# A top-k attention kernel whose fold takes one operand of its maximum from PSUM, with the second heads' keys stored tail first

## The chip, the cores and the metric

The kernel runs on one core of one Trainium2 chip. The metric is the device time of one execution in microseconds. Before the change the median of three runs is 1749.21 us (1747.92 to 1749.37). The engines are called as the profile calls them: PE (TensorE, matmuls; PEld is its weight load), DVE (VectorE), ACT (ScalarE), POOL (GpSimd) and SP (the queue that issues the transfers).

## The reference

Eight batches of eight heads, 576 positions, head size 64, fp32. The first block is attention that keeps the 32 largest scores of each row; the second is a mixer over positions of rank 32, and an MLP of width 2048 over channels.

```
scores = scale * q @ k.T
kth    = np.partition(scores, -32, axis=-1)[..., -32:-31]
scores = np.where(scores >= kth, scores, -1e9)
attn   = softmax(scores)                     # sum + 1e-9 below
x      = (attn @ v), heads side by side      # (8, 576, 512)
u      = x + (x.T @ U @ V).T
out    = u + relu(u @ w_ch1) @ w_ch2
```

## The kernel before, in words

**Pairs and chunks.** Two heads make a pair: 32 pairs `g`, four of each batch. A pair's 576 query rows are cut into five chunks `t`: four of 128 rows, in which both heads' scores lie side by side (2 x 576 columns), and a tail, in which the 64 last rows of one head stand above those of the other (576 columns). That gives 160 steps `n`. The positions of a head are kept as 512 (`MAIN`) and 64 (`TAIL`); `HALF` is 288.

**Loads.** `load(g)` fetches q, k and v on SP. From the sixth pair on (`blocked(g)`, `g > 4`) q and k are laid down in blocks of 32 so that one DVE transpose of 32 x 32 blocks, L290, makes `qkT` (heads on the two halves of the partitions, positions along the columns). Earlier pairs are turned by PE.

**Scores.** `scores(g, t)` multiplies by halves of 288 keys. A chunk of 128 rows uses two PSUM tiles `sc` of two banks each (L335, four matmuls): the first holds keys 0 to 287 of both heads, the second 288 to 575. Three ACT copies (L346, L347, L348) move them to `Ssb`, since head one's 64 last keys are put ahead of its first 512: head nought lies at columns 0 to 575, head one's tail at 576 to 639, its rest behind it. A tail chunk takes one tile, four matmuls of 64 rows (L323) and one copy (L330). `ps_s` has two such tiles in all, so a chunk's scores wait until the readers of the chunk before have let go of the tiles.

**The fold.** From the fifth pair on `fold` and `split` (both through `pair`) cut the search in two: POOL adds the two halves of each head's row as 32-bit words (L370), DVE takes their maximum (L372, `upper`), POOL subtracts that from the sum (L373), which leaves the minimum (`lower`). `front` then searches both: the 16 largest of `lower` join `upper` (L412 to L416), and `upper`, 304 wide, gives the 32 largest by MAX8 and MATCH_REPLACE8 (L426, L438, L443).

**After the search.** ACT makes `gap` (L468), POOL subtracts it (L471) so that what is under the threshold falls away, ACT takes the exponential and its sum (L377). For PV the probabilities have to be turned: in the first chunks by PE (`turns`, L526, L531), later by DVE in blocks (L498) and a way through DRAM, `away`, back as `PT` (L504, L508); `values` multiplies (L560, L564, L550). `mixed` applies the rank-32 mixer (L596, L608, L610), and `mlp` the two MLP products (L633, L652).

**What sets the order.** The program is written out by hand for all engines, and each engine runs its list in order. The MLP of one batch is a list of fillers: `fill()` puts a measured share of its matmuls between the attention's steps of the next batches. In a step `n` the scores and the POOL addition of `n + 1` come first, DVE's maximum for `n + 1` (`split`) after two rounds of the search for `n`, then the blocks of `n - 1`; PE's products with V follow in the step after. The weights arrive as 64-bit words and are joined meanwhile, by ACT (L174 to L178), DVE (L186) and POOL (L187, L189), up to about 310 us.

Of the kernel before, what the change touches and what calls it, by code (L numbers as in the profile page):

```python
# [12 lines left out]
ALU = mybir.AluOpType  # L13
# [13 lines left out]
def kernel(  # L27
# [28 lines left out]
    nc = tc.nc  # L56
    B, H, S, D = q.shape
# [5 lines left out]
    NT, TAIL = 4, 64  # L63
    MAIN = NT * P
    HALF = S // 2
# [10 lines left out]
    BLK = 32  # L76
# [49 lines left out]
    def rows(t):  # L126
        return P if t < NT else TAIL

    def cols(t):
        return slice(t * P, t * P + rows(t))  # L130
# [4 lines left out]
    def half(h):  # L135
        return slice(h * D, (h + 1) * D)
# [77 lines left out]
    raws, parts, passes = [], [], []  # L214
# [17 lines left out]


    raw, qkTs, S2s, uTs, XTs, dens = {}, {}, {}, {}, {}, {}
    probs, PTs, folds = {}, {}, {}

    def load(g):
        b, h0 = g // NPAIR, 2 * (g % NPAIR)
        ld = loads.tile([P, 2 * S], F32, tag="ld", name="ld")
        if blocked(g):  # L240
            for i, src in enumerate((q, k)):
                for a in range(4):
                    ds = src[b, h0 + a // 2, :, a % 2 * BLK : (a % 2 + 1) * BLK]
                    to = ld[a * BLK : (a + 1) * BLK, i * S : (i + 1) * S]
                    nc.sync.dma_start(
                        to[:, 0:MAIN].rearrange("i (t m d) -> i t m d", t=NT, d=BLK),
                        ds[0:MAIN].rearrange("(m i t) d -> i t m d", i=BLK, t=NT),
                    )
                    nc.sync.dma_start(
                        to[:, MAIN:S].rearrange("i (m d) -> i m d", d=BLK),  # L250
                        ds[MAIN:S].rearrange("(m i) d -> i m d", i=BLK),
                    )
            raw[g] = ld
        else:
            tiles = []
            ends = ld[:, 2 * MAIN : 2 * S].rearrange("p (h d) -> p h d", h=2)
            for j, src in enumerate((q, k)):
                t = ld[:, j * MAIN : (j + 1) * MAIN].rearrange("p (t h d) -> p t h d", t=NT, h=2)
                for i in range(2):
                    queue = nc.scalar if g == 0 and i else nc.sync  # L260
                    queue.dma_start(
                        t[:, :, i, :],
                        src[b, h0 + i, 0:MAIN, :].rearrange("(p t) d -> p t d", t=NT),
                    )
                tiles.append(t)
            for i, src in enumerate((q, k)):
                nc.sync.dma_start(
                    ends[half(i)], src[b, h0 : h0 + 2, MAIN:S, :].rearrange("h p d -> p h d")
                )
            raw[g] = tiles, ends  # L270
        va, vd, vt = (a[g % NV] for a in (vas, vds, vts))
        for i in range(2):
            nc.sync.dma_start(
                va[:, i], v[b, h0 + i, 0:MAIN, :].rearrange("(p t) d -> p t d", t=NT)
            )
            nc.sync.dma_start(vd[half(i), half(i)], v[b, h0 + i, MAIN:S, :])
        nc.sync.dma_start(vt[TAIL:P], v[b, h0 : h0 + 2, MAIN:S, :].rearrange("h p d -> p h d"))

    def blocked(g):

        return g > NPAIR
# [26 lines left out]
    def scores(g, t):  # L310

        qkT = qkTs[g]
        S2 = attn.tile([P, 2 * (S + TAIL)], F32, tag="Ssb", name="Ssb", bufs=4)
        n = 2 if t < NT else 1
        probs[g, t] = S2
        S2s[g, t] = S2[:, 0 : n * S].rearrange("p (c n) -> p c n", c=n)
        if t == NT:
            sc = ps_s.tile([P, 2, 512], F32, tag="sc", name="sc")  # L320
            for i in range(2):
                for h in range(2):
                    nc.tensor.matmul(  # L323
                        sc[half(h), i, 0:HALF],
                        lhsT=qkT[half(h), 0, cols(t)],
                        rhs=qkT[half(h), 1, i * HALF : (i + 1) * HALF],
                        start=True,
                        stop=True,
                    )
            nc.scalar.copy(S2[:, 0:S].rearrange("p (i n) -> p i n", i=2), sc[:, :, 0:HALF])  # L330
            return
        scs = [ps_s.tile([P, 2, 512], F32, tag="sc", name="sc") for _ in range(2)]
        for i, sc in enumerate(scs):
            for h in range(2):
                nc.tensor.matmul(  # L335
                    sc[:, h, 0:HALF],
                    lhsT=qkT[half(h), 0, cols(t)],
                    rhs=qkT[half(h), 1, i * HALF : (i + 1) * HALF],
                    start=True,
                    stop=True,  # L340
                )

        main = S2.rearrange("p (h n) -> p h n", h=2)
        last = S2[:, MAIN : MAIN + 2 * TAIL].rearrange("p (h n) -> p h n", h=2)
        copy = nc.vector.tensor_copy if g + t == 0 else nc.scalar.copy
        copy(main[:, :, 0:HALF], scs[0][:, :, 0:HALF])  # L346
        nc.scalar.copy(main[:, :, HALF:MAIN], scs[1][:, :, 0 : MAIN - HALF])  # L347
        nc.scalar.copy(last, scs[1][:, :, MAIN - HALF : HALF])  # L348

    def fold(g, t):  # L350

        if NPAIR <= g < NP:
            upper = attn.tile([P, 2, HALF + TOPK // 2], F32, tag="upper", name="upper")
            lower = attn.tile([P, 2, HALF], F32, tag="lower", name="lower", bufs=1)
            folds[g, t] = upper, lower
            pair(g, t, 0)

    def split(g, t):

        if (g, t) in folds:  # L360
            pair(g, t, 1)

    def pair(g, t, stage):
        S2 = S2s[g, t]
        n = S2.shape[1]
        upper, lower = folds[g, t]
        top, bottom = upper[:, 0:n, 0:HALF], lower[:, 0:n].bitcast(U32)
        a, b = S2[:, :, 0:HALF], S2[:, :, HALF:S]
        if stage == 0:
            nc.gpsimd.tensor_tensor(bottom, a.bitcast(U32), b.bitcast(U32), ALU.add)  # L370
        else:
            nc.vector.tensor_tensor(top, a, b, ALU.max)  # L372
            nc.gpsimd.tensor_tensor(bottom, bottom, top.bitcast(U32), ALU.subtract)  # L373

    def weigh(chunk, E, nmax, total=None):
# [349 lines left out]
    def fill(k=1):  # L725
# [3 lines left out]
        for _ in range(k):  # L729
# [5 lines left out]
            while due > 0:  # L735
# [6 lines left out]
                else:  # L742
                    due -= done

    load(0)
    next_params(1)
    t = 0
    for _ in prep(0):
        pass
    scores(0, 0)  # L750
    turning = ready = iter(())
    fronts = {}
    for n in range(STEPS + 2):
        g, t = divmod(n, CH)
        if n < STEPS:
            if t == 0 and g + 1 < NP:
                load(g + 1)
            if t == 1 and g + 1 < NP:
                ready = prep(g + 1)
            fronts[n] = front(g, t)  # L760
            next(fronts[n])
        here, last = fronts.get(n, iter(())), fronts.pop(n - 1, iter(()))
        if n >= ALONE - 1 and n <= ALONE:

            if n < ALONE:
                next(last)
                values(*divmod(n - 3, CH))
                list(turning)
                next(here)
                next(last)  # L770
                scores(*divmod(n + 1, CH))
                fold(*divmod(n + 1, CH))
                values(*divmod(n - 2, CH))
            list(turns(*divmod(n - 1, CH)))
            values(*divmod(n - 1, CH))
            if n < ALONE:
# [7 lines left out]
                continue  # L784
            fill()
            scores(*divmod(n + 1, CH))
            fold(*divmod(n + 1, CH))
            next(here)
# [111 lines left out]
```

## Time and profile before

| | us |
|---|---|
| median of three runs | 1749.21 |
| profiled execution | 1745.95 |
| its span, first to last instruction | 1744.1 |
| PE busy | 1638.1 |
| DVE busy | 1515.5 |
| ACT busy | 1030.4 |
| POOL busy | 973.2 |

The span lies 1.85 us below the profiled execution's own time. The first 200 us are attention alone (the first batch), the last 140 the MLP of the last batch alone; between them all engines work on both. In the views below a group's line gives the engine, the operation, what it writes and reads, how often, its busy time and the mean of one in ns, and behind the second bar the engine's idle time ahead of it with what ended it. A line in order of time gives start and duration in us; the bracket at its end is the idle time before it and who ended it. A busy PE is not PE at its peak, because the ends of matmuls are modelled.

### The profile page before, as it was taken

The numbers are of one execution on the slowest core, as the hardware profiler recorded it, in microseconds if no ns is written. First come the engines' busy times: TensorE is split into PE (matmuls) and PEld (weight loads), VectorE is DVE, ScalarE is ACT, GpSimd is POOL, SyncE is SP. The second block draws the span as 40 slices with busy tenths as digits, with TensorE's granted clock in tenths as the row PEclk, the third lists the DMA queues.
The fourth block names the chain that finished last, engine by engine and source line by source line (L and its number), as shares of the span: only waits on it lengthen the run. The fifth ranks groups of instructions, "written<-read, shape, count | busy, mean of one in ns | idle before, by whom it ended". The sixth has DMA issues, their size and how long they took to land.

```text
span 1744.1 us, 29711 instructions
## 1 busy us (share of the span) xinstructions
PE 1638.1 (94%) x9435; PEld 1202.4 (69%) x9435; DVE 1515.5 (87%) x4358; ACT 1030.4 (59%) x2690; POOL 973.2 (56%) x759
## 2 busy tenths in 40 slices
PE   4576789999999999999999999999999999999999
PEld 2444556677667776678767776678767776678677
DVE  7999889899999999999999999999999999993000
ACT  4888787665656666565656656565656666563100
POOL 4778787656555555656555555656555555652000
PEclk7678899999999999999999999999999999999999
DMA  3332222344444443444444444444444444422010
GB/s 89 89 93 82 71 72 60 70 111 112 112 109 122 107 117 101 116 107 112 109 111 120 103 113 106 116 113 112 109 112 123 105 111 105 121 85 82 3 16 13
DMA packets 275837, 167.36 MB, mean 96 GB/s; under 512 B 173920, under 2 KB 260192, under 8 KB 275680
## 3 DMA queue, kind: packets, MB, share of 16 engines
q1 hardware_dynamic: 274624, 165.20, 36.4%
q8 instruction: 74, 1.21, 0.3%
q14 instruction: 83, 0.68, 0.1%
q10 hardware_dynamic: 1056, 0.26, 0.1%
HBM read 101.42 MB, written 63.96 MB: 95 GB/s over the span
## 4 chain that ended last, share of the span: by engine, by line
PE 73%; DVE 16%; ACT 3%; DMA 3%; POOL 3%; issue 2%; SPq 1%; POOLq 0%; DVEq 0%; ACTq 0%
PE mm L652 26%; PE mm L633 23%; PE sc L335 6%; PE O L564 6%; DVE m L443 5%; DVE hT L438 3%; DVE upper L438 2%; DMA PT<-away 2%; PE sc L323 2%; DVE first L426 2%; PE O L550 2%; PE up L608 1%; PE tp L531 1%; PE O L560 1%; PE tp L526 1%
## 5 line engine op out<-in xcount | busy, mean ns | idle before, releaser
L652 PE MATMUL mm<-hT,w 128*128 128x256 f32 (+1 forms) x2048 | 544.6, 410 | 0.7 <-ACT hT L645 0.7
L633 PE MATMUL mm<-uT,w 128*128 128x256 f32 (+1 forms) x2048 | 540.2, 411 | 0.0
L471 POOL TENSOR_TENSOR Ssb<-Ssb,E 128x576 f32<-128x576 f32 x271 | 379.4, 1418 | 270.5 <-ACT E L468 269.9
L633 PEld LDWEIGHTS mm<-uT,w 128*128 128x128 f32 x2048 | 376.1, 192 | 100.0 <-issue 13.3
L652 PEld LDWEIGHTS mm<-hT,w 128*128 128x128 f32 x2048 | 373.6, 192 | 95.2 <-issue 11.7
L443 DVE MAX8 m<-upper 128x8 f32<-128x304 f32 x756 | 323.9, 466 | 2.9
L373 POOL TENSOR_TENSOR lower<-lower,upper 128x576 uint32<-128x576 uint32 (+1 forms) x140 | 180.5, 1289 | 137.2 <-DVE upper L372 130.5
L377 ACT ACTIVATE Ssb<-Ssb,nmax 128x576 f32<-128x576 f32 x286 | 222.6, 783 | 17.2 <-POOL Ssb L448 9.2
L370 POOL TENSOR_TENSOR lower<-Ssb 128x576 uint32<-128x576 uint32 (+1 forms) x140 | 194.8, 1392 | 59.3 <-DVE first L426 18.3
L438 DVE MATCH_REPLACE8 upper<-m,upper 128x304 f32<-128x304 f32 x504 | 227.6, 459 | 0.0
L645 ACT ACTIVATE hT<-mm 128x320 f32<-128x320 f32 (+1 forms) x256 | 105.8, 413 | 201.1 <-PE mm L633 198.7
L468 ACT ACTIVATE E<-Ssb,least 128x576 f32<-128x576 f32 x271 | 197.9, 769 | 5.2
L335 PE MATMUL sc<-qkT 64*128 64x288 f32 x1024 | 167.7, 448 | 9.3 <-ACT Ssb L346 8.5
L564 PE MATMUL O<-PT,va 128*64 128x128 f32 x2048 | 144.4, 285 | 9.8 <-DMA PT<-away 9.5
L498 DVE STREAM_TRANSPOSE y<-Ssb 128x512 f32<-128x512 f32 x208 | 138.5, 694 | 8.2 <-ACT Ssb L377 7.4
L335 PEld LDWEIGHTS sc<-qkT 64*128 64x128 f32 x1024 | 91.9, 194 | 71.3 <-issue 27.8
L412 DVE MAX8 upper<-lower 128x8 f32<-128x288 f32 x252 | 103.0, 445 | 41.0 <-POOL lower L373 41.0
L372 DVE TENSOR_TENSOR upper<-Ssb 128x576 f32<-128x576 f32 (+1 forms) x140 | 123.7, 884 | 11.6 <-ACT Ssb L348 11.0
L564 PEld LDWEIGHTS O<-PT,va 128*64 128x64 f32 x2048 | 113.0, 140 | 27.0 <-DMA PT<-away 12.2
L665 DVE TENSOR_TENSOR oT<-uT,mm 128x320 f32<-128x320 f32 (+1 forms) x8 | 3.6, 455 | 140.8 <-PE mm L652 140.8
L346 ACT COPY Ssb<-sc 128x576 f32<-128x576 f32 x127 | 80.6, 635 | 71.4 <-PE sc L335 69.9
L573 ACT COPY XT<-O 128x128 f32<-128x128 f32 x128 | 34.2, 267 | 143.1 <-PE O L564 143.1
(95 smaller groups left out, 2233.8 us busy)
## 6 DMA issues: line engine op xcount, KB each, us to landing
away<-y SPq DMA_DIRECT2D x416, 128.0 KB, 2.4
PT<-away SPq DMA_DIRECT2D x104, 512.0 KB, 3.3
raw<-in_moe_w_ch_dram SPq DMA_DIRECT2D x32, 512.0 KB, 3.8
va<-in_v_dram SPq DMA_DIRECT2D x64, 128.0 KB, 2.2
out_dram<-ob SPq DMA_DIRECT2D x57, 128.0 KB, 2.0
ld<-in_q_dram SPq DMA_DIRECT2D x108, 64.0 KB, 2.6
ld<-in_k_dram SPq DMA_DIRECT2D x108, 64.0 KB, 2.3
ld<-in_q_dram SPq DMA_DIRECT2D x108, 8.0 KB, 2.2
```

What stands on the lines that cost most here:

```text
L335: nc.tensor.matmul(sc[:, h, 0:HALF], lhsT=qkT[half(h), 0, cols(t)], rhs=qkT[half(h), 1, i * HALF : (i + 1) * HALF], start=True, stop=True,)
L370: nc.gpsimd.tensor_tensor(bottom, a.bitcast(U32), b.bitcast(U32), ALU.add)
L373: nc.gpsimd.tensor_tensor(bottom, bottom, top.bitcast(U32), ALU.subtract)
L377: nc.scalar.activation(E, chunk, AF.Exp, bias=nmax, scale=SCALE, accum_out=total)
L438: nc.vector.match_replace(nxt, ms[c], curs[c], NEG)
L443: nc.vector.max(ms[c], curs[c])
L468: nc.scalar.activation(gap, chunks[c], AF.Relu, bias=least[:, c : c + 1], scale=-WIDEN)
L471: nc.gpsimd.tensor_tensor(chunks[c], chunks[c], gap, ALU.subtract)
L498: nc.vector.transpose(y[:, :, h].rearrange("p r c j -> p c r j"), E2[:, a : a + MAIN].rearrange("p (c r j) -> p c r j", c=NT, r=4),)
L564: nc.tensor.matmul(O[half(h)], lhsT=va[:, h, j, :], rhs=PB[:, h, j] if shared(g, t) else PT[:, NT * h + j], start=False, stop=(j == NT - 1),)
L633: nc.tensor.matmul(ph[:, 0:w], lhsT=w1[:, cc, f * P : (f + 1) * P], rhs=uT[:, cc, lo:hi], start=(cc == 0), stop=(cc == NC - 1),)
L652: nc.tensor.matmul(po[:, 0:w], lhsT=w2[:, f, c * P : (c + 1) * P], rhs=hTs[f][:, 0:w], start=(f == 0), stop=(f == NF - 1),)
```

## The change

Four things are edited, all of them from the sixth pair on, apart from the last, which starts with the fifth pair's tail.

- `load` stores the keys of a pair's second head tail first: its 64 last keys at columns 0 to 63, the other 512 behind them. The queries stay.
- `scores` for 128 rows swaps the halves of the second head: the first tile holds keys 0 to 287 of head nought and stored keys 288 to 575 of head one, the second tile the other two. So each tile goes to `Ssb` in one copy of 576 columns (`ends_of`: quarters 0 and 3, or 1 and 2 of the row), and the three copies become two.
- The tail chunk wants the keys of both heads in one order, so head one's last product is cut in two, 224 and 64 columns: five matmuls for four.
- `fronts_of` keeps the first score tile, in PSUM, and the DVE maximum reads its first operand from there; the second is still read from `Ssb`, and so are both operands of POOL's addition. For tail chunks it is the first half of their one tile.

The score tile is then let go by DVE's maximum, no longer by ACT's copy. The products for the second tile of the next chunk wait for DVE where they waited for an earlier PE product or nothing of their own.

```diff
@@ load
+                    lead = TAIL if i and a >= 2 else 0
                     nc.sync.dma_start(
-                        to[:, 0:MAIN].rearrange("i (t m d) -> i t m d", t=NT, d=BLK),
+                        to[:, lead : lead + MAIN].rearrange("i (t m d) -> i t m d", t=NT, d=BLK),
                         ds[0:MAIN].rearrange("(m i t) d -> i t m d", i=BLK, t=NT),
                     )
+                    end = 0 if lead else MAIN
                     nc.sync.dma_start(
-                        to[:, MAIN:S].rearrange("i (m d) -> i m d", d=BLK),
+                        to[:, end : end + TAIL].rearrange("i (m d) -> i m d", d=BLK),
@@ scores
+        def product(out, h, lo, hi):
+            nc.tensor.matmul(
+                out,
+                lhsT=qkT[half(h), 0, cols(t)],
+                rhs=qkT[half(h), 1, lo:hi],
+                start=True,
+                stop=True,
+            )
+
         if t == NT:
             sc = ps_s.tile([P, 2, 512], F32, tag="sc", name="sc")
             for i in range(2):
                 for h in range(2):
-                    nc.tensor.matmul(
...
+                    lo = i * HALF + (TAIL if h and blocked(g) else 0)
+                    hi = min(lo + HALF, S)
+                    product(sc[half(h), i, 0 : hi - lo], h, lo, hi)
+                    if hi - lo < HALF:
+                        product(sc[half(h), i, hi - lo : HALF], h, 0, TAIL)
             nc.scalar.copy(S2[:, 0:S].rearrange("p (i n) -> p i n", i=2), sc[:, :, 0:HALF])
+            fronts_of[g, t] = sc[:, 0:1, 0:HALF]
             return
         scs = [ps_s.tile([P, 2, 512], F32, tag="sc", name="sc") for _ in range(2)]
         for i, sc in enumerate(scs):
             for h in range(2):
-                nc.tensor.matmul(
...
+                part = 1 - i if h and blocked(g) else i
+                product(sc[:, h, 0:HALF], h, part * HALF, (part + 1) * HALF)
+        if blocked(g):
+            for i, sc in enumerate(scs):
+                nc.scalar.copy(ends_of(S2, i), sc[:, :, 0:HALF])
+            fronts_of[g, t] = scs[0][:, :, 0:HALF]
+            return
...
+    def ends_of(S2, i):
+
+        parts = S2[:, 0 : 4 * HALF].rearrange("p (a n) -> p a n", a=4)
+        return parts[:, 1:3] if i else parts[:, 0:4:3]
+
@@ pair
         a, b = S2[:, :, 0:HALF], S2[:, :, HALF:S]
+        if t < NT and blocked(g):
+            a, b = (ends_of(probs[g, t], i) for i in range(2))
         if stage == 0:
             nc.gpsimd.tensor_tensor(bottom, a.bitcast(U32), b.bitcast(U32), ALU.add)
         else:
-            nc.vector.tensor_tensor(top, a, b, ALU.max)
+            nc.vector.tensor_tensor(top, fronts_of.pop((g, t), a), b, ALU.max)
             nc.gpsimd.tensor_tensor(bottom, bottom, top.bitcast(U32), ALU.subtract)
```

More of the change, by code (lines that the diff above doesn't have):

```diff
@@ L234 @@
     raw, qkTs, S2s, uTs, XTs, dens = {}, {}, {}, {}, {}, {}
-    probs, PTs, folds = {}, {}, {}
+    probs, PTs, folds, fronts_of = {}, {}, {}, {}
     def load(g):
@@ L322, in scores @@
                 for h in range(2):
-                    nc.tensor.matmul(
[L324 to L329, printed above, removed]
+                    lo = i * HALF + (TAIL if h and blocked(g) else 0)
[3 more added lines that the diff above has]
+                        product(sc[half(h), i, hi - lo : HALF], h, 0, TAIL)
             nc.scalar.copy(S2[:, 0:S].rearrange("p (i n) -> p i n", i=2), sc[:, :, 0:HALF])
+            fronts_of[g, t] = sc[:, 0:1, 0:HALF]
             return
@@ L334, in scores @@
             for h in range(2):
[L335 to L341, printed above, removed]
+                part = 1 - i if h and blocked(g) else i
[5 more added lines that the diff above has]
+            return
         main = S2.rearrange("p (h n) -> p h n", h=2)
```

## The prediction

> **What bounds the kernel now.** I read the page's busy shares and slices first, then the same by stretches, because a share over the whole span mixes stages. From the page:
>
> ```profile
> span 1744.1 us, 29711 instructions
> ...
> PE 1638.1 (94%) x9435; PEld 1202.4 (69%) x9435; DVE 1515.5 (87%) x4358; ACT 1030.4 (59%) x2690; POOL 973.2 (56%) x759
> ...
> PE   4576789999999999999999999999999999999999
> ...
> DVE  7999889899999999999999999999999999993000
> ...
> PE 73%; DVE 16%; ACT 3%; DMA 3%; POOL 3%; issue 2%; SPq 1%; POOLq 0%; DVEq 0%; ACTq 0%
> ```
>
> TensorE and VectorE both look full; the chain of waits (last line) gives TensorE 73% of the span. The busy time by stretches (PE, PEld, DVE, ACT, POOL, clock, DMA) says where each one rules:
>
> ```profile
> 249.00:420.00 171.00, 159.68 (x949) 116.32 (x947) 160.47 (x464) 113.97 (x294) 114.26 (x88) 0.98 0.35 89
> 420.00:600.00 180.00, 177.94 (x1054) 129.78 (x1053) 173.45 (x525) 109.97 (x296) 103.75 (x80) 1.00 0.43 109
> 600.00:1600.00 1000.00, 996.04 (x5874) 736.94 (x5873) 943.01 (x2835) 604.54 (x1621) 574.71 (x445) 1.00 0.43 110
> 284.00:292.00 8.00, 6.11 (x24) 3.92 (x25) 8.00 (x21) 4.66 (x15) 7.84 (x7) 0.57 0.20 66
> ```
>
> The sixth pair's first scores are at 249 us, so nothing before 239 (the fifth pair's tail) can change. From 600 to 1600 TensorE idles 4 us in 1000, and after 1600 only TensorE's MLP is left: there VectorE's time is covered. What can be won from 249 on is TensorE's own idle time: 17 us, of which 13 lie between 249 and 445, plus 284 to 292, where the clock fell to 0.57.
>
> What the change touches, in the groups by form:
>
> ```profile
> L372 DVE TENSOR_TENSOR upper<-Ssb 128x576 f32<-128x576 f32 x112 | 106.7, 953 | 11.6 <-ACT Ssb L348 11.0
> L370 POOL TENSOR_TENSOR lower<-Ssb 128x576 uint32<-128x576 uint32 x112 | 172.2, 1537 | 52.7 <-DVE first L426 18.3 <-ACT Ssb L348 15.1 <-issue 5.7
> L347 ACT COPY Ssb<-sc 128x448 f32<-128x448 f32 x128 | 68.7, 537 | 3.7 <-PE sc L335 3.7
> L348 ACT COPY Ssb<-sc 128x128 f32<-128x128 f32 x128 | 36.0, 281 | 0.0
> L372 DVE TENSOR_TENSOR upper<-Ssb 128x288 f32<-128x288 f32 x28 | 17.0, 607 | 0.0
> L665 DVE TENSOR_TENSOR oT<-uT,mm 128x320 f32<-128x320 f32 x4 | 2.0, 488 | 89.3 <-PE mm L652 89.3
> L346 DVE COPY Ssb<-sc 128x576 f32<-128x576 f32 x1 | 0.8, 757 | 1.4 <-PE sc L335 1.4
> L665 DVE TENSOR_TENSOR oT<-uT,mm 128x256 f32<-128x256 f32 x4 | 1.7, 422 | 51.5 <-PE mm L652 51.5
> ```
>
> The maximum's mean of 953 ns hides two populations. The order of time shows a blocked one, and three of the TensorE gaps that can be won:
>
> ```profile
> 267.55 1.28 POOL L189 TENSOR_TENSOR w<-w,raw 128x512 uint32<-128x512 uint32 x1
> 267.67 1.77 DVE L372 TENSOR_TENSOR upper<-Ssb 128x576 f32<-128x576 f32 x1
> 285.77 1.03 PE L596 MATMUL pT<-x,U 128*32 128x128 f32 x10 [3.19 <-ACT PT L527]
> 362.02 1.09 PE L564 MATMUL O<-PT,va 128*64 128x128 f32 x16 [1.24 <-DMA PT<-away]
> 412.00 1.09 PE L564 MATMUL O<-PT,va 128*64 128x128 f32 x16 [2.97 <-DMA PT<-away]
> ```
>
> A POOL add that starts just before the maximum holds it until the add ends (267.55 + 1.28 = 268.83, and the maximum ends 0.6 us later). Without a POOL neighbour it takes 0.74 us. From 249 to 445 nine of 16 full-size maxima are over 0.9 us; their excess over 0.755 us is 8.0 us. After 445 most are 0.74 and the excess is 11.3 us in 92, mainly at a pair's first chunk.
>
> [...] MAX8, one input, 0.46 us beside busy and idle POOL alike; a maximum with one PSUM and one SBUF input beside a busy POOL no run here shows. [...]
>
> **The change part by part.** *Maximum.* PSUM operand: L665 has this form, 422 ns for 256 and 488 for 320 elements, 66 ns per 64. So 576 elements take 488 + 4 x 66 = 752 ns and 288 take 455; the copy from PSUM (757) agrees. Unblocked from SBUF it takes 0.74, so the operand itself costs nothing; what goes is the block: 8.0 + 11.3 us in 108 full-size ones and 4.2 in 28 tails, 23.5 us of VectorE. Bounds: 0 if the block stays, 23.5 if it goes; I take the latter. POOL, blocked in its turn (L370 1.94 us instead of 1.41), gains some.
> *Copies.* 537 + 281 become one of 576, 635: 0.18 us per chunk less, 20 us of ScalarE in 108, hidden under its 40% idle except around 250 to 290, where ScalarE is on the chain.
> *Loads* have the same number and sizes, at other columns; the transposed q and k need no other work. Nothing.
> *Tail scores.* One more 64-column product for each of 27 pairs, on the engine that bounds. The columns of each head stay 288 + 288. The two heads run side by side now (eight passes in 1.12 us), so the extra passes cost between nothing and two lone ones: load 133 ns + 64 columns at the 288-per-240-ns rate, 53 ns, twice, 0.37. I take 0.1: 2.7 us; range 0 to 10.
> *New wait.* The score tile read by the maximum is released by VectorE. TensorE's next chunk needs it for its second pair of products, and behind it in the queue stand all MLP products. Today the maximum ends 2.9 to 7.9 us before that point from 290 on; at 269 and 280 it would be 0.5 and 0.2 us late, but those two maxima were blocked by 1.0 us. Nothing, as long as the block goes.
>
> What reaches the end, gap by gap:
> - 249 to 292: a POOL add held up by 0.5 us, then the maxima at 267.7 and 278.3 by 1.0 each, let VectorE run 1.5 us earlier at 271 and 2.5 at 281. TensorE's gaps at 273.2 and 274.8 (0.72 + 0.28, behind ScalarE work that waits for VectorE) close: 1.0. The gap at 285.8 shortens by 1.0 more (ScalarE's queue, not VectorE, is late next). With 2.2 us idle the clock should hold; the 5.7 us at half speed then take 2.8 less.
> - 312: 0.37, a POOL subtraction blocked by the maximum.
> - 335 to 412: the chain is VectorE without a break, with blocked maxima at 342.9, 360.6 and 379.6 (0.6 + 1.1 + 0.7), a tail (0.35) and 0.5 carried in by POOL: 3.3 of the 5.5 us of gaps at 362, 371 and 412.
> - 439: 1.63 idle behind POOL's queue; VectorE is 1.1 earlier (408.9: 1.87). 1.1.
> - Later gaps on the transposes' return at 459, 566, 764, 960, 1156 and 1594: 0.12, 0.31, 0.74 of 1.93, 0.53, 0.50, 0.57 of 0.73; in most a blocked maximum (1.39 to 1.65) stood ahead of those transposes: 2.8.
>
> Sum: 1.0 + 1.0 + 2.8 + 0.4 + 3.3 + 1.1 + 2.8 = 12.4 won, 2.7 lost: 9.7. The profiled execution took 1745.95 us (1744.1 span + 1.85 around it): 1736.3. The median of the runs stands 3.3 higher, 1739.5; I say 1740, with half a microsecond off for gains that don't add.
>
> **The rivals.** *Mostly covered:* gaps move rather than close, another engine or transfer ending the same waits; the transfers behind the gaps take 3 to 4 us each whatever VectorE does. For it: by gaps, half of the sum hangs on two or three places. It leaves 2 to 4 us of gain, less 2.7: 1747 to 1749.
> *The block stays:* the change then doesn't do what it says[...]. VectorE gains nothing and the split product costs 2.7: about 1751. [...]
> *Slower:* reading one half from two PSUM banks while a ScalarE copy runs is slow. VectorE idles 57 us in the 1000 after 600, 0.56 us per chunk of 9.8 us, and the maximum averages 0.82 there; it decides from an average of 1.38, full-size ones near 1.55. At 1.8 us (average 1.6) VectorE becomes the bound by 0.24 us in each of some 120 chunks: 29 us, 1775. L665 and the copy speak against it.
> *Dear split:* 0.37 per tail, 10 us, eats most of the gain: 1747.
>
> **How the numbers follow.** Main case 0.66 (own range 1735 to 1745), covered 0.16, block stays 0.07, dear split 0.04, slower 0.05, more than summed 0.02. Leaving out the slower and block cases and the fringes, 8 in 10 lie in 1735 to 1748.5. A measurement tells 0.2%, 3.5 us, from no change: the main case and a bit of the covered one are faster, 0.72; most of covered, dear split and block, 0.20; the rest slower, 0.08.
>
> **What would show it.** Maxima at 0.75 us throughout, tails 0.46; POOL's L370 group at 1.41; no half clock near 285; TensorE's idle time from 249 to 445 down from 13 to about 7 us; tail scores 0.1 us longer; no TensorE wait on the maximum. The prediction is wrong if maxima beside POOL adds still last 1.2 us or more, if gaps reappear behind ScalarE or transfers, or if TensorE waits for the maximum.

## The result and the profile after

The changed kernel takes 1742.65 us (median of four runs, 1741.95 to 1743.93) where the kernel before takes 1749.29 (1747.92 to 1750.12): 6.6 us less, a ratio of 0.9964 with a 95% interval of 0.9946 to 0.9981. The forecast was 1740 with a range of 1735 to 1748.5. The profiled execution took 1742.03 us, its span 1740.2. Line numbers behind `scores` are 17 higher than before: L372 is now L389, L370 is L387, L498 is L515, L564 is L581, L652 is L669.

From the page of the changed kernel (span, busy time of each engine, the chain that ended last):

```profile
span 1740.2 us, 29711 instructions
...
PE 1634.9 (94%) x9489; PEld 1208.1 (69%) x9489; DVE 1494.1 (86%) x4358; ACT 1023.9 (59%) x2582; POOL 956.7 (55%) x759
...
PE 78%; DVE 11%; DMA 3%; ACT 3%; POOL 1%; issue 1%; SPq 1%; POOLq 0%; DVEq 0%; ACTq 0%
```

VectorE has lost 21.4 us of busy time and GpSimd 16.5, and the end came only 3.9 us earlier in the profiled executions. TensorE has 54 more matmuls (9489 for 9435), since each of the 27 added products shows as two matmuls; of three copies per chunk ScalarE has two left. TensorE still bounds; its share of the chain has risen from 73 to 78%, VectorE's has fallen from 16 to 11%.

By stretches, with the columns as before (PE, PEld, DVE, ACT, POOL, clock, DMA share, GB/s):

```profile
249.00:420.00 171.00, 164.46 (x1007) 121.74 (x1006) 156.87 (x488) 117.96 (x290) 117.36 (x92) 1.00 0.36 92
...
600.00:1600.00 1000.00, 994.77 (x5896) 741.42 (x5893) 928.55 (x2823) 596.03 (x1533) 557.52 (x442) 1.00 0.43 110
284.00:292.00 8.00, 7.24 (x44) 5.21 (x45) 6.65 (x19) 4.88 (x13) 7.28 (x6) 1.00 0.21 66
```

The first row gained: TensorE is busy for 164.5 of the 171 us (159.7 before) and the clock is at 1.00 (0.98). In the last row, 284 to 292 us, the clock went from 0.57 to 1.00. From 600 to 1600 VectorE has 14.5 us less to do, and TensorE is no busier than it was (994.8 for 996.0).

The groups by form that the change touches:

```profile
L389 DVE TENSOR_TENSOR upper<-sc,Ssb 128x576 f32<-128x576 f32 x108 | 80.3, 744 | 10.4 <-ACT Ssb L349 10.2
L389 DVE TENSOR_TENSOR upper<-sc,Ssb 128x288 f32<-128x288 f32 x28 | 12.3, 440 | 0.0
L387 POOL TENSOR_TENSOR lower<-Ssb 128x576 uint32<-128x576 uint32 x112 | 159.0, 1420 | 61.2 <-ACT Ssb L349 23.5 <-DVE upper L455 8.3 <-issue 7.9
```

The maximum reads `sc` now, and its mean of 744 ns (953 before, two populations) is one population: the longest of the 108 takes 0.76 us, where before single ones took up to 2.01. POOL's addition, which was held up in its turn, fell from 1537 to 1420 ns. The order of time shows the two side by side:

```profile
276.12 1.30 POOL L189 TENSOR_TENSOR w<-w,raw 128x512 uint32<-128x512 uint32 x1
276.30 0.73 DVE L389 TENSOR_TENSOR upper<-sc,Ssb 128x576 f32<-128x576 f32 x1
```

The addition runs from 276.12 to 277.42, the maximum starts inside it and ends inside it, at 277.03. Before, such a pair gave 1.77 us. Of the 108, 53 overlap an instruction of POOL, and the longest of these takes 0.76 us; the longest of the 55 others takes 0.75. Of the 112 before, the 53 that overlap one have a median of 1.21 us, and the longest of the 59 others takes 0.76.

TensorE's gaps, in order of time (the bracket is the idle time ahead and who ended it):

```profile
283.34 0.60 PE L613 MATMUL pT<-x,U 128*32 128x128 f32 x10 [1.54 <-ACT PT L544]
...
404.91 1.09 PE L581 MATMUL O<-PT,va 128*64 128x128 f32 x16 [1.12 <-DMA PT<-away]
...
1588.48 1.09 PE L581 MATMUL O<-PT,va 128*64 128x128 f32 x16 [2.27 <-DMA PT<-away]
```

The gap of 3.19 us is 1.54 now, with one of 0.76 at 285.5. The gap of 2.97 us at 412 is the one of 1.12 at 404.91; those of 1.24 and 1.34 became 0.83 and 0.92. The last line is the loss: at the very end of the attention a gap of 0.73 us became one of 2.27.

Where the time was won shows in the starts of the chunks' scores on TensorE. Both kernels do the same up to chunk 24, so the distance from there counts. The table holds one profiled execution of each kernel:

| chunks | stretch before, us | stretch after, us | won |
|---|---|---|---|
| 24 to 29 | 58.43 | 53.26 | 5.2 |
| 29 to 34 | 50.09 | 50.04 | 0.0 |
| 34 to 44 | 98.01 | 95.35 | 2.7 |
| 44 to 139 | 932.25 | 931.71 | 0.5 |
| 139 to the end | 365.67 | 369.40 | -3.7 |

8.4 us are won by chunk 139, almost all of it before 445 us, and 3.7 are given back at the end. The changed kernel's profiled execution also started chunk 24 0.8 us later, before anything of the change takes effect. So the table explains a difference of 3.9 us. The medians of the runs lie 6.6 us apart, because the profiled execution of the kernel before was 3.3 us faster than the median of its runs, and that of the changed kernel only 0.6.

### The profile page after: what moved, and what is told of

Its sections match the earlier page's. It is cut to its first block, busy times and chain, and to the rows that moved or that the text cites. A ratio compares the mean times of both kernels' runs of the same rounds, so it can differ in the third digit from the quotient of the medians.

```text
span 1740.2 us, 29711 instructions
## 1 busy us (share of the span) xinstructions
PE 1634.9 (94%) x9489; PEld 1208.1 (69%) x9489; DVE 1494.1 (86%) x4358; ACT 1023.9 (59%) x2582; POOL 956.7 (55%) x759
## 4 chain that ended last, share of the span: by engine, by line
PE 78%; DVE 11%; DMA 3%; ACT 3%; POOL 1%; issue 1%; SPq 1%; POOLq 0%; DVEq 0%; ACTq 0%
PE mm L669 27%; PE mm L650 26%; PE sc L322 8%; PE O L581 6%; DVE m L460 4%; DVE hT L455 4%; DMA PT<-away 2%; PE O L567 2%; PE up L625 2%; PE tp L548 1%; DVE first L443 1%; PE O L577 1%; PE tp L543 1%; DMA away<-y 1%; PE up L627 1%
## 5 line engine op out<-in xcount | busy, mean ns | idle before, releaser
L669 PE MATMUL mm<-hT,w 128*128 128x256 f32 (+1 forms) x2048 | 545.1, 411 | 0.0
L669 PEld LDWEIGHTS mm<-hT,w 128*128 128x128 f32 x2048 | 374.4, 192 | 94.7 <-issue 11.5
L390 POOL TENSOR_TENSOR lower<-lower,upper 128x576 uint32<-128x576 uint32 (+1 forms) x140 | 180.2, 1287 | 110.4 <-DVE upper L389 103.3
L387 POOL TENSOR_TENSOR lower<-Ssb 128x576 uint32<-128x576 uint32 (+1 forms) x140 | 181.5, 1296 | 69.5 <-ACT Ssb L349 23.5
L322 PE MATMUL sc<-qkT 64*128 64x288 f32 x1334 | 209.6, 437 | 8.6 <-ACT Ssb L356 7.8
L322 PEld LDWEIGHTS sc<-qkT 64*128 64x128 f32 x1334 | 115.4, 182 | 94.5 <-issue 42.6
L349 ACT COPY Ssb<-sc 128x576 f32<-128x576 f32 x216 | 127.1, 640 | 83.4 <-PE sc L322 82.1
L515 DVE STREAM_TRANSPOSE y<-Ssb 128x512 f32<-128x512 f32 x208 | 142.9, 702 | 22.8 <-ACT Ssb L394 20.9
L581 PE MATMUL O<-PT,va 128*64 128x128 f32 x2048 | 145.0, 285 | 8.5 <-DMA PT<-away 8.5
L581 PEld LDWEIGHTS O<-PT,va 128*64 128x64 f32 x2048 | 113.5, 141 | 25.5 <-DMA PT<-away 10.8
L455 DVE MATCH_REPLACE8 upper<-first,upper 128x304 f32<-128x304 f32 x252 | 114.0, 459 | 0.0
```

Of the source, the lines that this page charges most:

```text
L322: nc.tensor.matmul(out, lhsT=qkT[half(h), 0, cols(t)], rhs=qkT[half(h), 1, lo:hi], start=True, stop=True,)
L455: nc.vector.match_replace(nxt, ms[c], curs[c], NEG)
L515: nc.vector.transpose(y[:, :, h].rearrange("p r c j -> p c r j"), E2[:, a : a + MAIN].rearrange("p (c r j) -> p c r j", c=NT, r=4),)
L581: nc.tensor.matmul(O[half(h)], lhsT=va[:, h, j, :], rhs=PB[:, h, j] if shared(g, t) else PT[:, NT * h + j], start=False, stop=(j == NT - 1),)
L669: nc.tensor.matmul(po[:, 0:w], lhsT=w2[:, f, c * P : (c + 1) * P], rhs=hTs[f][:, 0:w], start=(f == 0), stop=(f == NF - 1),)
```

## The experiments

Each edit stands on the changed kernel unless it says otherwise. The changed kernel and the three with another operand of the maximum ran on one chip (the kernel before: 1747.59 us median there); the three copies, the cut products, the other order and the last chunk without its trip on another (1747.86); the three with extra products on a third (1748.29); so times are compared within a group, and the ratios, which are to the kernel before on the same chip, across them. None of these kernels leaves any work out.

### Which part brings the time, and where

The changed kernel once more, without an edit, as the measure for the three behind it.

> The changed kernel itself, beside its parts on one chip, so that they can be compared with it. Every theory expects 1742 to 1744 us, 5 to 7.5 below the kernel before.

1742.69 us (1741.15 to 1743.75), ratio 0.9968 (0.9956 to 0.9981): the result again. In this execution too the stretch from 284 us has lost its gap of 3.2 us, though a half clock (a stretch in which TensorE's granted clock is 0.5) of 3.4 us is still there at 285.6, where it was 6.8 us before. Whether it goes altogether is not certain from one execution to the next: in the nine profiled executions here whose maxima read PSUM in this stretch it lasts 0 us in four, 3.4 in four and 6.8 in one.

**The maximum from SBUF again,** all else as changed (two copies, the keys tail first, the split products):

```diff
-            nc.vector.tensor_tensor(top, fronts_of.pop((g, t), a), b, ALU.max)
+            nc.vector.tensor_tensor(top, a, b, ALU.max)
```

> The maximum reads both halves from SBUF again; layout, swapped halves, two copies and the split product stay. Theory (the gain is the end of the blocking between VectorE's maximum and POOL): the blocked maxima of 1.2 to 2.0 us are back, TensorE's idle time from 249 to 445 us is back near 13 us, and the time at 1748 to 1750. Rival (the gain comes from two copies in place of three, which let POOL and VectorE start earlier): 1743 to 1745. If the split product cost its 0.1 us each, 1750 to 1752.

1749.65 us, ratio 1.0011 (1.0003 to 1.0019). The whole gain goes with this one operand: 7.0 us to the kernel above. In order of time in this kernel:

```profile
267.96 1.28 POOL L189 TENSOR_TENSOR w<-w,raw 128x512 uint32<-128x512 uint32 x1
268.08 1.78 DVE L389 TENSOR_TENSOR upper<-Ssb 128x576 f32<-128x576 f32 x1
```

The block is back (941 ns in the mean, 1.78 us beside an addition), and with it POOL's 1535 ns per addition and TensorE's gap of 3.19 us at 286. TensorE's idle time from 249 to 445 us is 11.2 us, less than the 13 that were expected (the changed kernel has 8.2). So the operand takes the block away, and the rest of the change brings nothing in sum (the ratio is a little above 1). The rest is not without effect, though: before 445 us the full-size maxima exceed 0.755 us by 6.2 us in all, where they did by 8.0 before the change, so some of the blocks are gone or shorter when only the rest is changed.

**From PSUM in the first four of the pairs only,** and in the later ones only:

```diff
-            nc.vector.tensor_tensor(top, fronts_of.pop((g, t), a), b, ALU.max)
+            front = fronts_of.pop((g, t), a)
+            nc.vector.tensor_tensor(top, front if g <= 2 * NPAIR else a, b, ALU.max)
```

(the second kernel with `g > 2 * NPAIR`; `NPAIR` is 4, so the line falls at chunk 45, about 445 us.)

> The maximum reads PSUM for pairs up to the ninth only (chunks up to some 450 us), SBUF afterwards. Theory (what reaches the end is TensorE's idle time before 445 us, the rest of VectorE's gain is covered): 1742 to 1745, most of the gain. Rival (VectorE's time counts wherever it is saved; 15 of 23.5 us are saved after 445): 1747, a third of the gain.

> The other part: SBUF for pairs up to the ninth, PSUM from the tenth on. Theory: TensorE waits for VectorE only now and then there, in all under 2 us: 1747 to 1750. Rival (VectorE's time counts wherever it is saved): 1745.

First pairs: 1743.28 us, ratio 0.9975 (0.9964 to 0.9986). Later pairs: 1749.06 us, ratio 1.0010 (1.0001 to 1.0018). The first lies 0.6 us from the whole change, the second 0.6 us from the kernel that reads SBUF throughout, both inside the intervals. The stretches of the second show why:

```profile
249.00:420.00 171.00, 160.24 (x954) 117.64 (x953) 156.79 (x461) 113.30 (x280) 115.27 (x88) 0.98 0.34 89
...
600.00:1600.00 1000.00, 995.43 (x5899) 741.92 (x5899) 933.41 (x2834) 598.57 (x1539) 562.05 (x445) 1.00 0.43 110
```

From 249 to 420 us TensorE is where it was before the change (160.2), and from 600 on VectorE's 10 us less than before (933.4 for 943.0) do nothing for it. As far as these runs can tell (the intervals are some 2 us wide to each side), the gain is made by 21 of the 136 maxima, those of the stretch in which VectorE is on the path; the 115 others only add to VectorE's spare time.

Which place within that stretch brings it is shown for the first one only. Over the thirteen profiled executions of this document, chunk 24 to 29 takes 53.1 to 56.6 us in the nine that read PSUM there and 58.4 to 60.1 in the four that don't. Chunk 34 to 44 takes 95.0 to 97.6 us with the operand from PSUM and 96.0 to 98.7 without, and the two kernels of this pair stand the other way round than the operand would have it: first pairs, which reads PSUM there, takes 97.63 us, and later pairs, which reads SBUF there, 96.02. The gap at the end of this stretch, first pairs and then later pairs:

```profile
405.60 1.94 PE L582 MATMUL O<-PT,va 128*64 128x128 f32 x16 [2.38 <-DMA PT<-away]
```

```profile
411.75 1.09 PE L582 MATMUL O<-PT,va 128*64 128x128 f32 x16 [1.84 <-DMA PT<-away]
```

The gap that was 2.97 us before the change is 1.84 with the operand in SBUF, and 2.38 with a half clock behind it in an execution with the operand in PSUM. So of the 2.7 us that the table gives to chunk 34 to 44, about 2 also come without the operand, in that execution.

### What the rest costs

**Three copies again,** the second tile's cut in 224 and 64 columns:

```diff
-                nc.scalar.copy(ends_of(S2, i), sc[:, :, 0:HALF])
+                if i == 0:
+                    nc.scalar.copy(ends_of(S2, i), sc[:, :, 0:HALF])
+                    continue
+                cut = MAIN - HALF
+                nc.scalar.copy(ends_of(S2, i)[:, :, 0:cut], sc[:, :, 0:cut])
+                nc.scalar.copy(ends_of(S2, i)[:, :, cut:HALF], sc[:, :, cut:HALF])
```

> The second score tile goes to SBUF in two copies again (2 x 224 and 2 x 64 columns), so that there are three; the maximum still reads PSUM. Theory (the end of the blocking carries the gain): within 1 us of the changed kernel, 1742.5 to 1744. Rival (the two copies carry it): 1747 to 1749.

1742.51 us, ratio 0.9975 (0.9966 to 0.9983). TensorE's idle time from 249 to 445 us is 8.3 us, as in the changed kernel (8.2). What the third copy costs ScalarE is covered, around 250 to 290 too.

**All products of the second head cut in two,** in the 128-row chunks as well, 216 more of them:

```diff
-                product(sc[:, h, 0:HALF], h, part * HALF, (part + 1) * HALF)
+                lo = part * HALF
+                if h and blocked(g):
+                    product(sc[:, h, 0 : HALF - TAIL], h, lo, lo + HALF - TAIL)
+                    product(sc[:, h, HALF - TAIL : HALF], h, lo + HALF - TAIL, lo + HALF)
+                else:
+                    product(sc[:, h, 0:HALF], h, lo, lo + HALF)
```

> In all chunks of 128 rows from the sixth pair on, both products of the second head are cut into 224 and 64 columns as in the tails: 216 more products on the engine that bounds. By the predicted 0.1 us each 1764; by the 7 ns that the tail's product group grew by in the profile of the changed kernel 1744 to 1745; by the upper bound of 0.37 us each 1822.

1757.61 us, ratio 1.0056 (1.0044 to 1.0068), 15.1 us above the kernel with three copies on the same chip, which has the changed kernel's time. From the first product of a chunk's scores to TensorE's next work it takes 1349 ns instead of 1172, so 177 for two cuts and 89 for one; times 216 that is 19.1 us, of which some 3 went into idle time (6.0 us from 249 to 445 and 4.9 behind it, for 8.2 and 5.8). The tail's cut, with 64 rows and the two heads side by side, shows 1126 ns in the changed kernel for 1118 before: 8 ns, in 27 tails 0.2 us. A cut product has no price of its own; it costs eleven times as much in one shape as in the other.

### The new wait and VectorE's order

**The blocks ahead of the maximum.** The transposes `y` of chunk `n - 1`, with which the trip through DRAM begins, come before the maximum of chunk `n + 1`; the score tile is let go later:

```diff
-        split(*divmod(n + 1, CH))
         if away:
             blocks(*divmod(n - 1, CH))
+        split(*divmod(n + 1, CH))
```

> The block transposes of the chunk before come ahead of the maximum in VectorE's list, so that their way through DRAM starts up to 0.75 us earlier and the maximum ends up to 1.4 us later. If TensorE's gaps on the way back (8.5 us in all in the changed kernel) hang on when VectorE starts it: 1738 to 1741, and TensorE does not wait for the later maximum. If the transposes stand ready behind ScalarE's exponential, VectorE idles longer and the maximum and the POOL subtraction come late: 1743 to 1748.

1745.00 us, ratio 0.9988 (0.9981 to 0.9996): 2.5 us above the kernel with three copies on the same chip, which has the changed kernel's time. No gap of TensorE over 80 ns ends on the maximum here either, so the release of the tile has room to spare. What went up is TensorE's idle time behind 445 us, 9.0 for 5.8, all on `PT<-away`. By the groups, first this kernel, then the changed one (VectorE's transposes):

```profile
L515 DVE STREAM_TRANSPOSE y<-Ssb 128x512 f32<-128x512 f32 x208 | 142.9, 707 | 37.6 <-ACT Ssb L394 36.0
```

```profile
L515 DVE STREAM_TRANSPOSE y<-Ssb 128x512 f32<-128x512 f32 x208 | 142.9, 702 | 22.8 <-ACT Ssb L394 20.9
```

Put first, the transposes find their operand not yet written: VectorE stands for 37.6 us ahead of them instead of 22.8, waiting for ScalarE's exponential, and POOL's subtractions (L390) wait for the maximum for 213 us instead of 90. With the maximum first that waiting time is used. This wait also fits with how little VectorE's gain behind 445 us is worth: it was 8.2 us before the change (9.0 in the kernel with the block back) and is 22.8 in the changed one, in which VectorE comes earlier to an operand that ScalarE delivers no sooner.

### The end, where time is given back

The gap of 2.27 us at 1588 ends on a trip: four transfers take the probabilities to DRAM (`away<-y`), one brings them back turned (`PT<-away`). The transfers of this window, before and after; first the kernel before, 1586.7 to 1594 us, then the changed one, 1579.6 to 1588.4 (queue, packets, MB, share of the engines; then issues with the size and the median us from issue to landing):

```profile
q1 hardware_dynamic: 991, 1.18, 55.1%
...
away<-y SPq DMA_DIRECT2D x4, 128.0 KB, 2.4
```

```profile
q8 instruction: 1, 0.02, 0.7%
...
away<-y SPq DMA_DIRECT2D x4, 128.0 KB, 3.4
```

Same transfers, same bytes, but in the changed kernel one packet of kind "instruction" lies among them, and the way out takes 3.4 us instead of 2.4 (the way back 3.7 and 3.6). These packets hold 16 KB each; there are 74 before and 75 after, and in the traces one comes for every 250 or so weight loads and matmuls of TensorE (median 253 before, 252 after). With the 166 semaphore instructions and 3 drains counted that the trace also has in TensorE's stream, the median is 256 in both. What these packets carry was not shown; they are called instruction packets below. The change adds 27 products to TensorE, each two loads and two matmuls, so 108 instructions, and moves the places of these packets. With 148 more, 256 in all, they would by that spacing lie where they lay before:

```diff
+    idle = ps_t.tile([P, P], F32, tag="tp", name="idle")
+    for _ in range(37):
+        nc.tensor.matmul(idle[0:BLK, 0:8], lhsT=ident[0:BLK, 0:BLK], rhs=ident[0:BLK, 0:8], start=True, stop=True)
```

> The changed kernel with 37 tiny extra products (32 rows, 32 x 8) before the first step, into a tile that nobody reads: 148 more instructions on TensorE, which with the 108 of the change make 256, the spacing at which the instruction transfers come in the traces. Nothing is left out. Fetch theory (the last gap before 1600 us comes from an instruction transfer that falls into the last trip of the probabilities through DRAM): the transfers stand again where they stood before the change, so the last gap is at most 0.9 us instead of 2.0 to 2.35, no half clock follows it, and the time is 1740 to 1741.5 us although the 37 products cost about 1 us near the start. Rival (the gap comes from where the change puts VectorE and ScalarE at the end): gap of 2.0 to 2.35 us and 1743 to 1744.5 us.

And the kernel **before**, with 27 of these products and nothing of the change:

```diff
+    idle = ps_t.tile([P, P], F32, tag="tp", name="idle")
+    for _ in range(27):
+        nc.tensor.matmul(idle[0:BLK, 0:8], lhsT=ident[0:BLK, 0:BLK], rhs=ident[0:BLK, 0:8], start=True, stop=True)
```

> The kernel before with 27 of the same tiny products before the first step: 108 more instructions on TensorE, as many as the change adds, and nothing else of the change. Nothing is left out. Fetch theory: an instruction transfer falls into the last trip through DRAM as in the changed kernel, the last gap grows from 0.73 to about 2 us or more, and the time is 1750 to 1752 us. Rival: last gap 0.6 to 0.9 us, time 1747.5 to 1749.5 us.

The same windows around the last trip, the changed kernel with 37 products first, then the kernel before with 27:

```profile
q1 hardware_dynamic: 990, 1.18, 59.9%
...
away<-y SPq DMA_DIRECT2D x4, 128.0 KB, 2.4
```

```profile
...
q8 instruction: 1, 0.02, 0.7%
...
away<-y SPq DMA_DIRECT2D x4, 128.0 KB, 3.4
```

And TensorE in order of time at the return of that trip, again the changed kernel with 37 first, then the kernel before with 27:

```profile
1587.07 1.09 PE L581 MATMUL O<-PT,va 128*64 128x128 f32 x16 [0.68 <-DMA PT<-away]
```

```profile
1597.15 1.09 PE L564 MATMUL O<-PT,va 128*64 128x128 f32 x16 [2.08 <-DMA PT<-away]
```

The 37 products take 4.1 us of TensorE at 10 us, not the 1 us that was expected, but chunk 24 starts at 239.7 us, no later than in the changed kernel (240.4). The packet came and went as foretold, with it the slow way out (2.4 and 3.4 us) and the gap (0.68 and 2.08 us). That the instruction packet in the last trip makes the gap is shown in both directions, in one profiled execution each, and the other traces agree: in the eight profiled executions with such a packet inside the last trip it takes 8.6 to 9.0 us and the gap is 2.0 to 2.4; in the three without one it takes 7.1 to 7.3 us and the gap is 0.7 or less. In the changed kernel the sixteen matmuls behind the gap took 5.41 us instead of 3.72, at half clock; in these two kernels they take 3.72, so gap and clock together cost 3.3 us there.

By the runs it is less clear. With 37 products: 1740.89 us, ratio 0.9959 (0.9946 to 0.9971), inside what was expected, but its interval overlaps that of the changed kernel. The kernel before with 27: 1748.51 us, ratio 1.0003 (0.9995 to 1.0011). The expected 1.7 to 3.7 us more did not come. In its profiled execution the clock held after the gap, and the other gaps changed places: 11.6 us of idle time from 249 to 445 for 13.0, 6.1 behind it for 4.4. So a shift of the instruction packets moves time between trips; over a whole execution it summed to nothing that could be measured here. It is then no proof of why the kernels with the block back lie 0.1% above the kernel before. Both have the long last gap (2.35 and 2.05 us) and a half clock of 3.4 us behind it, which would do, but that stays open.

**The last chunk without the trip:** TensorE turns the probabilities of the last 128-row chunk; without and with the 37 products:

```diff
-        return t < NT and g * CH + t >= ROUNDED
+        return t < NT and ROUNDED <= g * CH + t < STEPS - 2
```

> The probabilities of the last 128-row chunk are turned by TensorE, not through DRAM. The changed kernel's profile shows 2.27 us of idle TensorE there and a half clock for 3.4 us after it. If these stand in most executions: 1739.5 to 1741.5. If the profiled execution was an odd one: 1742 to 1743.5, since TensorE gets 0.9 us more work.

> The 37 extra products, and the last 128-row chunk turned by TensorE instead of going through DRAM. Nothing is left out. Fetch theory: the last trip is gone in both this and the kernel without the extra products (1741.3 us), so the place of the transfers no longer matters at the end: 1740 to 1742.5 us, no gain over it. If the extra products help in another way, it is under 1740.

1741.31 us, ratio 0.9959 (0.9946 to 0.9972), and 1740.49 us, ratio 0.9956 (0.9943 to 0.9968). The last gap is gone in both. They are the fastest kernels here by their medians, as is the one with 37 products, but none of the three can be told from the changed kernel (0.9968, 0.9956 to 0.9981).

## Why the prediction was right, step by step

*The block goes, the operand costs nothing:* right, though that the block goes was an estimate, which the trace of before did not show. 0.73 to 0.76 us in all 108, 0.43 to 0.45 in the tails, and putting the SBUF operand back returns it.

*249 to 292:* right in the gaps, and lucky in the clock. 4.8 us were predicted (gaps 2.0, clock 2.8), and 5.2 came from chunk 24 to 29 in the profiled execution; in the next one of the same kernel 3.6 came. The step had 2.2 us of idle time left and let the clock hold, which was an estimate: in the trace of before a half clock of 6.8 us begins within the gap of 3.19 us, and none follows the one of 2.97 us. Some 2.2 to 2.3 us were left in both executions; in one the half clock stays away, in the other it lasts 3.4 us. Where the idle time falls decides that (see the last section), and the prediction had no way to know it.

*335 to 412:* right in number, not shown in cause. 3.3 predicted, 2.7 measured; the three gaps shrank from 5.55 to 2.87. But in the two kernels with all of the change except the operand in this stretch they shrank as well, to 3.62 and 3.13, so most of it does not hang on the operand. Shorter blocks and moved instruction packets can both have done that: the kernel before with 27 products, where only these packets are moved, has 4.44 us of such gaps from 360 to 420. How much each did stays open.

*312:* wrong, 0.4 predicted. The gap is 0.37 as before.

*439:* wrong, 1.1 predicted; it is 1.63 us before and after, also in the kernel with the block back (1.63) and in those with extra products (1.64). The step read "idle behind POOL's queue" and took VectorE for what made POOL late. The chain of waits of the changed kernel from 425 to 440 us shows another:

```profile
425.67 0.23 PE tp L717 x2
...
425.93 0.37 ACT ob L719
...
426.56 1.44 ACT E L485 x2
...
429.14 1.06 POOL Ssb L488
430.20 1.36 POOL lower L387
431.56 0.69 POOL oT L685
...
432.30 0.44 PE tp L717 x2
```

It begins with TensorE's own transposes, goes through ScalarE's and POOL's queues and comes back to TensorE; VectorE is not in it. A VectorE that is earlier can't shorten it. The fault of the step was to go back one releaser and not the whole way round.

*Later gaps on the transposes' return:* wrong, 2.8 predicted. From 44 to 139 0.5 us was won; TensorE's idle time behind 445 us rose from 4.4 to 5.8. One part of the error is the cause: a blocked maximum stood ahead of those transposes, but a trip is late mostly where an instruction packet crosses it: over the kernel before, trips with one inside take 8.2 us (median of 30) and trips without 7.1 (74), in the changed kernel 8.1 and 7.1; of its nine gaps over 80 ns behind 445 us eight belong to trips with such a packet inside (five of seven before). The other part is the end, which the sum had as a gain of 0.57 us and which lost 3.7.

*The split product:* mis-sized, 0.1 us each, 2.7 in all; 8 ns, 0.2 in all. The upper bound of 0.37 was four times what a cut costs even where the second head's product stands alone (0.089).

*No new wait, copies hidden:* right, by the gaps and the two experiments.

The sum was 9.7 us and the runs gave 6.6. The first two places hold 7.9 of the 8.4 us won by chunk 139, and the kernel with the operand in the first four pairs alone shows that the result is made before 445 us. What is missing are the small gains (312, 439, later, 4.3 predicted and 0.5 measured) and the end, with the cheap split against them. By the two profiled executions, 4.7 us are left from chunk 24 on (5.2, 2.7 and 0.5, less 3.7); the other 1.9 of the 6.6 lie in how far these two executions stood from their medians, and no place can be named for them. So the mechanism was right, while it is in part luck that the number came as near as 2.7 us: several terms were too high and one loss was not in the sum. Of the rivals, "mostly covered" describes the kernel from 445 us on, and not the part before it.

## What to carry to other kernels

Price a saving on an engine by the stretch in which that engine is on the path: 21 of 136 maxima carried the gain here, as far as the runs can tell it. When a gap is to close, follow its releasers until the chain comes back to the engine that waits; if the engine you relieve isn't on that round, the gap stays. And where a short transfer's trip has less slack than about 1 us (the way out took 3.4 us here with an instruction packet in it and 2.4 without), its lateness may depend on the mere count of instructions ahead of it, so a gap that appears after an edit elsewhere can be tried with a few dozen tiny instructions before it is put down to the edit.

## What the runs showed of the hardware that was not expected

- A transfer lands later where an instruction packet comes among its packets. A 16 KB packet (eight in ten of them take 0.9 to 1.4 us) inside the last trip made four 128 KB transfers land after 3.4 us instead of 2.4, and over all trips of the changed kernel those with such a packet inside take 8.1 us where the others take 7.1. The 75 of them are only 0.3% of the engines' time on the page, and most of the late trips were theirs.
- The length of a gap doesn't say whether it halves TensorE's clock; where it falls does. In each of the thirteen traces all half clocks begin at whole steps of 3.413 us from each other. With the idle time between matmuls added up step by step from 249 to 1605 us, no step at full clock with less than 1.64 us of it is followed by a half clock, all ten with more than 2.0 us are, and of the nine between six are. A gap that lies across the border of two steps so counts in two parts:

| gap | us | idle in its steps, us | clock of the step behind |
|---|---|---|---|
| kernel before with 27 products, 439 us | 1.64 | 1.64 | half |
| last chunk without the trip, 283 us | 2.05 | 2.05 | half |
| changed kernel, 1588 us | 2.27 | 0.36 and 1.91 | half |
| kernel before with 27 products, 1597 us | 2.08 | 1.15 and 0.92 | full |
| three copies, 1589 us | 2.22 | 0.79 and 1.43 | full |

So a step of 3.413 us that was idle for 1.91 us, 56% of it, was enough in the changed kernel. What halves the clock was not shown beyond this.
- Cutting a matmul of 288 columns in 224 and 64 costs 89 ns where the profile gives the product as 64\*128 (the 128-row chunks: 1349 ns for 1172, two cuts) and 8 ns where it gives 64\*64 (the tails: 1126 ns for 1118, one cut).
